# Streaming-window attention and a channel mix on one core: sink scores in column tiles, small copies spread over engines, zero matmuls limited to the start

## The chip, the cores and the metric

The kernel runs on one core of one Trainium2 chip. The metric is the device time of one execution in microseconds (us). The engines are TensorE (PE, and PEld for its weight loads), VectorE (DVE), ScalarE (ACT), GpSimd (POOL) and SyncE (SP), which issues nearly all DMAs.

## The reference

Four batches, eight heads, 768 positions, head size 64. Each position attends to the 128 positions up to itself and to the first four positions of its batch (the sinks). The heads side by side give rows of 512 numbers, which go through a channel mix.

```python
scores = scale * np.matmul(q, k.transpose(0, 1, 3, 2))
keep = is_sink | in_window                       # pos < 4, or 0 <= rel < 128
a = np.exp(scores - max); a = a / (sum(a) + 1e-09)
x = np.matmul(a, v)                              # -> (B, S, 512)

xk = mu_k * x + (1.0 - mu_k) * x_prev            # x_prev: one position earlier
xr = mu_r * x + (1.0 - mu_r) * x_prev
k = np.maximum(xk @ w_k, 0.0)                    # 512 -> 1024
v = k * k @ w_v                                  # 1024 -> 512
r = 1.0 / (1.0 + np.exp(-(xr @ w_r)))            # 512 -> 512
return r * v
```

Inputs and output are float32; the kernel multiplies in bf16.

## The kernel before

The work is cut into 12 units `u`, each 256 positions of a batch: `b, T = divmod(u, 3)`. A unit passes through four functions. Names in brackets are the tiles and lines of the profile.

- `prepare(u)`: keys and queries are loaded in float32 (`ks`, `qs`), cast to bf16 (`kb`, `qb`, L526 and L529), transposed on TensorE (L550) and copied out of PSUM (`kt`, `qt`, L560). For later units (keys from unit 4, queries from unit 8) a DMA transposes instead (L537). Values are cast to `vb` (L575). For the first unit of a batch the keys of the four sinks are copied into `ksink` (L588), and their values, spread over partitions by a matmul (L594), into `vsink` (L598).
- `attend(u)`: sink scores (L611) for units with T > 0; window scores two head pairs at a time (L635), the two heads of a pair in the two 64-row halves of the array; exponentials (`e`, L657; `es`, L619); masks (L671); values (L682, L694); division by the sum (`rec`, L707; `x`, L710).
- `mix(u)`: x is transposed (L733) and copied out (`xt`, L744); the difference to the position before (`td`, L758); four `xk` and four `xr` (L768).
- `ffn(u)`: key products (L818), relu (`rl`, L827), its square (`kk`, L831), gates (L841) and tanh (`th`, L847), products with w_v (L859, for the last 128 rows L788), output (`ob`, L868) and its store (L875). The sigmoid is made from a tanh, and w_v is halved for it when it is cast.

Every piece of work is declared by `P.op(engine, cost, emit, ...)` with what it reads, writes, takes from a pool and holds. The pools of buffers (`ks`, `kt`, `e`, `bank`, ...) set how far ahead work may run. The order on each engine is written out by hand in `ORDER`, as numbers of operations. `Plan.schedule()` walks the five lists with the costs, chooses a buffer for each taking, and merges the lists into one program. It also finds stretches in which TensorE would wait and puts zero matmuls there (L879, on the tile `warm`), as long as its own clock is below `P.fill_until`. The engines themselves run their lists in order and wait on semaphores.

The weights w_k (halves a and b), w_r and w_v (halves a and b) are loaded once, in float32, into tiles of their own, and cast in ten pieces on VectorE (L503, L501). In SyncE's list the loads of unit 0 come first, then keys and queries of unit 1, both halves of w_k, values of unit 1, queries of unit 2, w_r, keys of unit 2, and then w_v's halves between queries and keys of unit 3.

Of the kernel before, what the change touches and what calls it, by code (L numbers as in the profile page):

```python
# [17 lines left out]
CAST = {"k": "ACT", "q": "ACT"}  # L18

CAST0 = {"k": "DVE", "q": "DVE"}  # L20
EVAC0 = {"k": "ACT", "q": "DVE", "x": "ACT"}
# [14 lines left out]
LOADS = ("kq0", "v0", "kq1", "wka", "v1", "wkb", "wr", "wva", "wvb")  # L36
WCAST = ("DVE",) * 10
VCAST = ("DVE", "POOL")
# [6 lines left out]
        92, 89, 98, 105, 95, 116, 108, 113, 128, 141, 124, 119, 131, 137, 103, 148, 134, 157,  # L45
        155, 168, 219, 211, 207, 212, 220, 208, 160, 176, 165, 171, 183, 189, 215, 193, 200,
        223, 180, 216, 225, 237, 298, 186, 290, 302, 291, 303, 299, 294, 248, 295, 227, 235,
        231, 263, 232, 228, 260, 306, 266, 318, 240, 256, 245, 251, 310, 276, 269, 311, 283,
        326, 329, 308, 321, 314, 343, 315, 370, 378, 352, 366, 371, 379, 332, 367, 374, 382,
        337, 375, 384, 359, 348, 386, 396, 387, 421, 390, 274, 444, 391, 452, 445, 453, 426,  # L50
        407, 448, 456, 394, 449, 457, 460, 399, 464, 404, 465, 415, 462, 410, 430, 472, 499,
        578, 437, 468, 474, 504, 469, 525, 583, 526, 537, 485, 538, 533, 509, 529, 534, 530,
        477, 553, 482, 488, 493, 545, 511, 564, 518, 549, 541, 546, 543, 550, 601, 609, 605,
        602, 556, 610, 606, 567, 631, 613, 561, 572, 614, 617, 587, 619, 621, 594, 629, 622,
        634, 625, 639, 626, 642, 677, 689, 678, 681, 663, 690, 682, 645, 707, 685, 650, 686,
        695, 701, 670, 718, 705, 702, 693, 697, 710, 698, 760, 715, 761, 756, 768, 757, 769,
        721, 726, 764, 742, 765, 772, 749, 740, 784, 780, 774, 781, 795, 834, 830, 835, 842,
        831, 787, 843, 838, 792, 798, 860, 776, 803, 816, 839, 777, 823, 846, 848, 854, 858,
        855, 871, 910, 918, 906, 911, 907, 850, 863, 851, 919, 868, 936, 874, 914, 879, 915,
        930, 892, 924, 899, 931, 926, 947, 934, 922, 944, 939, 927, 976, 972, 977, 984, 973,  # L60
        985, 950, 980, 955, 958, 981, 988, 990, 965, 992, 996, 993, 997, 1012, 1000, 1013, 1004,
        1001, 1005, 1008, 1016, 1009, 1020, 1018, 1021, 1028, 1024, 1029, 1025,
    ),
    "DVE": (
        70, 91, 88, 93, 97, 71, 94, 99, 100, 107, 112, 101, 123, 109, 114, 110, 118, 115, 120,
        125, 143, 121, 126, 146, 144, 78, 145, 150, 79, 151, 152, 81, 164, 154, 104, 159, 147,
        175, 170, 161, 80, 162, 177, 166, 178, 167, 172, 153, 173, 82, 83, 202, 195, 196, 210,
        69, 197, 203, 204, 198, 206, 84, 85, 205, 199, 214, 218, 239, 293, 301, 222, 86, 305,
        87, 255, 297, 250, 233, 244, 229, 241, 242, 257, 246, 247, 252, 258, 253, 325, 320, 278,
        312, 279, 285, 280, 287, 322, 286, 327, 323, 328, 331, 316, 281, 289, 288, 282, 354,  # L70
        333, 334, 336, 369, 373, 338, 355, 339, 377, 361, 381, 362, 356, 363, 388, 275, 357,
        392, 364, 365, 398, 358, 403, 447, 451, 414, 455, 400, 459, 401, 409, 405, 406, 466,
        416, 417, 411, 412, 432, 433, 434, 439, 441, 440, 435, 470, 442, 481, 476, 528, 436,
        510, 487, 492, 478, 532, 479, 483, 443, 489, 484, 494, 490, 495, 540, 555, 560, 513,
        536, 514, 520, 516, 515, 522, 521, 547, 551, 523, 571, 517, 566, 557, 558, 604, 524,
        568, 569, 562, 563, 573, 574, 608, 633, 612, 616, 589, 592, 590, 638, 623, 635, 591,
        596, 598, 597, 627, 636, 640, 641, 593, 599, 644, 600, 665, 649, 646, 680, 692, 647,
        684, 651, 652, 714, 666, 688, 709, 672, 667, 674, 703, 668, 675, 673, 711, 725, 699,
        712, 676, 716, 720, 669, 717, 722, 723, 727, 759, 728, 763, 744, 767, 745, 751, 771,
        746, 753, 752, 741, 786, 782, 747, 755, 791, 797, 788, 789, 833, 793, 799, 802, 794,  # L80
        800, 748, 804, 845, 805, 754, 837, 778, 841, 825, 818, 821, 819, 820, 826, 829, 827,
        867, 856, 862, 822, 878, 909, 864, 873, 865, 852, 913, 869, 870, 875, 876, 880, 828,
        881, 917, 921, 894, 943, 897, 932, 895, 938, 896, 901, 905, 902, 945, 903, 940, 941,
        928, 949, 946, 954, 904, 951, 952, 898, 956, 975, 957, 960, 979, 961, 963, 987, 962,
        983, 967, 969, 970, 968, 971, 994, 964, 998, 1003, 1007, 1015, 1011, 1022, 1030, 1026,
    ),
    "ACT": (
        67, 68, 90, 111, 106, 96, 122, 117, 127, 130, 136, 142, 129, 132, 133, 149, 138, 163,
        135, 158, 156, 169, 174, 221, 213, 182, 209, 188, 184, 190, 201, 194, 179, 185, 224,
        181, 217, 226, 238, 187, 243, 292, 262, 300, 304, 296, 254, 249, 236, 264, 259, 265,  # L90
        261, 307, 267, 319, 268, 324, 277, 270, 284, 342, 340, 309, 330, 335, 344, 345, 347,
        353, 372, 380, 368, 420, 425, 383, 376, 360, 498, 418, 349, 385, 397, 422, 503, 423,
        402, 496, 454, 427, 446, 413, 450, 395, 458, 408, 461, 501, 577, 582, 575, 463, 431,
        473, 500, 438, 579, 475, 480, 505, 584, 527, 486, 491, 535, 531, 539, 559, 554, 512,
        519, 565, 580, 542, 544, 653, 570, 655, 603, 611, 607, 657, 632, 615, 618, 588, 659,
        637, 630, 620, 731, 595, 735, 643, 648, 679, 664, 691, 683, 729, 713, 708, 687, 671,
        696, 733, 808, 724, 706, 694, 719, 806, 762, 810, 758, 770, 743, 766, 812, 750, 785,
        790, 775, 773, 801, 882, 796, 836, 832, 844, 866, 861, 840, 817, 824, 849, 847, 884,
        859, 888, 886, 872, 877, 912, 908, 942, 920, 916, 893, 937, 925, 900, 935, 948, 923,
        953, 978, 974, 986, 959, 989, 982, 991, 966, 1014, 1002, 1006, 1010, 1019, 1017,  # L100
    ),
    "POOL": (
        77, 72, 73, 75, 76, 74, 102, 139, 140, 191, 192, 271, 273, 272, 350, 351, 428, 506, 429,
        585, 507, 661, 508, 586, 662, 737, 738, 739, 814, 815, 890, 891,
    ),
    "SP": (
        1, 3, 0, 2, 4, 5, 6, 7, 8, 11, 9, 10, 16, 12, 15, 13, 20, 14, 19, 17, 18, 21, 22, 25,
        23, 234, 24, 30, 341, 28, 35, 346, 313, 29, 317, 26, 33, 27, 389, 38, 34, 40, 31, 419,
        424, 36, 393, 497, 230, 32, 502, 37, 41, 43, 576, 39, 467, 44, 45, 581, 46, 47, 656, 42,
        548, 51, 654, 471, 52, 660, 658, 49, 552, 628, 57, 50, 48, 55, 56, 53, 730, 732, 736,  # L110
        58, 734, 54, 704, 61, 807, 811, 809, 813, 63, 700, 783, 64, 624, 62, 883, 59, 60, 885,
        889, 887, 857, 65, 853, 779, 66, 929, 933, 999, 995, 1023, 1031, 1027,
# [4 lines left out]
class Plan:  # L117
# [17 lines left out]
    def op(self, engine, cost, emit, rank, reads=(), writes=(), take=(), hold=(), port=False,  # L135
           lag=None, service=0.0, descs=128, mode=0):
        self.ops.append(dict(engine=engine, cost=cost, emit=emit, rank=rank, reads=list(reads),
                             writes=list(writes), take=list(take), hold=list(hold), port=port,
                             lag=90.0 if lag is None else lag, service=service, descs=descs, mode=mode))

    def schedule(self):
# [42 lines left out]
        while any(lines.values()):  # L184
# [35 lines left out]
            if o["service"]:  # L220

                descs = o["descs"]
# [9 lines left out]
                flying.append((dma, descs))  # L232
# [39 lines left out]
def kernel(  # L272
# [36 lines left out]
    for name in ("ks", "qs", "vs"):  # L309
        pool(name, 3, [128, 2, H, D] if name == "vs" else [128, H, 2, D], FP32)  # L310
    pool("kb", 3, [128, 2, H, D], BF16)
    pool("qb", 3, [128, 2, H, D], BF16)
    pool("kt", 4, [128, NP, 2, 128], BF16)
    pool("qt", 3, [128, NP, 2, 128], BF16)
# [5 lines left out]
    pool("xk", 3, [128, NC, 256], BF16)  # L320
    pool("xr", 3, [128, NC, 256], BF16)
    pool("kk", 2, [128, NF, 256], BF16)
    pool("rl", 4, [128, 2, 256], BF16)
    pool("th", 4, [128, Dm], FP32)
    pool("ob", 3, [128, Dm], FP32)
    pool("vb", 3, [128, 2, H, D + 1], BF16)
    buf = P.buf

    def tile1(shape, dtype, name):
        return const.tile(shape, dtype, name=name)  # L330


# [144 lines left out]
    def make_sinks():  # L477
        for t in vsink:
            nc.gpsimd.tensor_copy(out=t[0:32, :, D:D + 1], in_=hmask[:, :, D:D + 1])
# [451 lines left out]
```

## Time and profile before

| | |
|---|---|
| median of 4 runs | 172.4 us (172.18 to 172.5) |
| the profiled execution | 172.5 us |
| its span, first to last instruction | 170.8 us |
| granted TensorE clock | 1.00 |
| busy: PE, DVE, ACT, POOL | 162.3, 148.6, 132.5, 24.3 us |
| zero matmuls (L879) | 42, 13.4 us busy |
| sink scores (L611) | 32 matmuls in 8 units |
| value casts on GpSimd (L575) | 22, 811 ns each |
| moved by DMA | 33.8 MB, 198 GB/s over the span |

The profile is of one execution. Busy time of an engine is the union of its instructions' times. Matmuls are pipelined, so an instruction's duration (273 ns for a 256-column matmul) is longer than its distance to the next one; the work on TensorE is better read from the distance of starts. The chain of work that ended last is followed back from the end: each piece is what released the next one, or came before it on its engine. In the timeline, brackets give idle time before an instruction and what ended it.

### The profile page before, as it was taken

Reading aid. Unit: us, or ns where it says so; the run is one execution under the profiler, and the core shown is the slowest. Engines: PE = TensorE matmul, PEld = TensorE weight load, DVE = VectorE, ACT = ScalarE, POOL = GpSimd, SP = SyncE. Lnnn points to the kernel's source line nnn. Section 1 sums busy time; section 2 is a strip of 40 time slices with the busy share of each in tenths; the row PEclk is TensorE's granted clock in tenths of the full one; section 3 lists DMA queues with packets and bytes.
Section 4 is the critical chain, followed back from the end, with each engine's and each line's share of the span. In section 5 each row is a group of like instructions: output and inputs, shape, how many; then the busy total and the mean of one; then the engine's idle time right before and its main releaser. Section 6 shows DMA issues by size and latency. Waiting matters only on the chain.

```text
span 170.8 us, 4214 instructions
## 1 busy us (share of the span) xinstructions
PE 162.3 (95%) x1603; PEld 108.3 (63%) x1624; DVE 148.6 (87%) x372; ACT 132.5 (78%) x219; POOL 24.3 (14%) x47
## 2 busy tenths in 40 slices
PE   7998997899999999999999999999999999999992
PEld 2445585475758567667658668577585775684751
DVE  3496999899899778999999999998999988999632
ACT  3169988899999999999879979978887938654330
POOL 6130040004400020122201200212000402000000
PEclk9999999999999999999999999999999999999999
DMA  4999989998969999999948999977999674030203
GB/s 104 234 273 378 254 268 324 360 311 195 298 175 214 225 255 255 164 258 184 235 86 150 264 230 224 226 135 196 144 271 203 115 212 130 0 125 1 108 15 123
DMA packets 82803, 33.82 MB, mean 198 GB/s; under 512 B 64736, under 2 KB 77280, under 8 KB 82784
## 3 DMA queue, kind: packets, MB, share of 16 engines
q1 hardware_dynamic: 81728, 33.56, 84.3%
q8 instruction: 12, 0.20, 0.5%
q10 hardware_dynamic: 1056, 0.00, 0.3%
q14 instruction: 7, 0.06, 0.1%
HBM read 24.12 MB, written 6.29 MB: 178 GB/s over the span
## 4 chain that ended last, share of the span: by engine, by line
PE 79%; SPq 12%; DMA 5%; issue 1%; ACT 0%; DVE 0%
PE bank L818 23%; PE bank L859 23%; PE bank L841 11%; PE sc L635 6%; DMA ks<-in_k_dram 5%; PE bank L694 5%; SPq L377 5%; SPq L360 4%; PE bank L733 3%; SPq L397 3%; PE bank L682 2%; PE bank L550 2%; PE bank L611 2%; PE bank L788 1%; PE bank L594 0%
## 5 line engine op out<-in xcount | busy, mean ns | idle before, releaser
L657 ACT ACTIVATE e<-sc 128x1024 bf16<-128x1024 f32 (+1 forms) x48 | 44.9, 973 | 5.3 <-PE sc L635 5.3
L818 PE MATMUL bank<-xk,wk_sb 128*128 128x256 bf16 x384 | 49.0, 273 | 0.0
L859 PE MATMUL bank<-wv_h,kk 128*128 128x512 bf16 x173 | 45.4, 379 | 0.6
L818 PEld LDWEIGHTS <-wk_sb 128*128 128x128 bf16 x384 | 35.6, 98 | 7.2 <-issue 0.2
L827 ACT ACTIVATE rl<-bank 128x512 bf16<-128x512 f32 x48 | 27.5, 605 | 9.2 <-PE bank L818 8.6
L575 POOL CAST vb<-vs 128x512 bf16<-128x512 f32 x22 | 17.6, 811 | 111.9 <-DMA vs<-in_v_dram 111.9
L671 DVE TENSOR_TENSOR e<-e,mask 128x1024 bf16<-128x1024 bf16 (+1 forms) x48 | 31.0, 656 | 0.7 <-ACT e L657 0.7
L859 PEld LDWEIGHTS <-kk 128*128 128x128 bf16 x184 | 16.7, 98 | 14.5 <-DVE kk L831 0.2
L841 PE MATMUL bank<-wr_sb,xr 128*128 128x512 bf16 x88 | 23.9, 379 | 0.8 <-DVE wr_sb L503 0.5
L831 DVE TENSOR_TENSOR kk<-rl 128x512 bf16<-128x512 bf16 x48 | 20.1, 432 | 4.6 <-ACT rl L827 4.4
L768 DVE SCALAR_TENSOR_TENSOR xr<-td,mu,xt 128x256 bf16<-128x256 bf16 x48 | 23.2, 499 | 0.1
L768 DVE SCALAR_TENSOR_TENSOR xk<-td,mu,xt 128x256 bf16<-128x256 bf16 x48 | 22.2, 489 | 0.2
L710 DVE TENSOR_TENSOR x<-bank,rec 128x256 bf16<-128x256 f32 x48 | 19.5, 416 | 0.6
L694 PE MATMUL bank<-vb,e 128*128 128x65 bf16 x352 | 18.9, 193 | 0.0
L694 PEld LDWEIGHTS <-e 128*128 128x128 bf16 x352 | 16.8, 97 | 2.8 <-DVE wk_sb L503 0.6
L847 ACT ACTIVATE th<-bank 128x512 f32<-128x512 f32 x24 | 14.1, 599 | 5.0 <-PE bank L841 4.8
L868 DVE SCALAR_TENSOR_TENSOR ob<-th,bank 128x512 f32<-128x512 f32 x23 | 15.6, 680 | 2.1 <-ACT th L847 1.7
L744 ACT COPY xt<-bank 128x512 bf16<-128x512 bf16 x24 | 14.1, 592 | 3.8 <-PE bank L733 3.5
L879 PE MATMUL bank<-warm 128*128 128x512 bf16 x42 | 13.4, 453 | 1.4 <-DVE warm L894 1.3
L841 PEld LDWEIGHTS <-xr 128*128 128x128 bf16 x96 | 9.0, 98 | 8.3 <-DVE wr_sb L503 0.4
L635 PE MATMUL sc<-qt,kt 64*128 64x128 bf16 (+1 forms) x256 | 14.0, 238 | 0.0
L682 PE MATMUL bank<-vsink,es 128*128 128x130 bf16 x64 | 12.5, 220 | 0.5 <-ACT rl L827 0.5
(54 smaller groups left out, 155.9 us busy)
## 6 DMA issues: line engine op xcount, KB each, us to landing
vs<-in_v_dram SPq DMA_DIRECT2D x24, 256.0 KB, 4.5
out_dram<-ob SPq DMA_DIRECT2D x23, 256.0 KB, 3.3
ks<-in_k_dram SPq DMA_DIRECT2D x18, 256.0 KB, 5.0
qs<-in_q_dram SPq DMA_DIRECT2D x7, 512.0 KB, 6.4
qs<-in_q_dram SPq DMA_DIRECT2D x10, 256.0 KB, 4.0
wk<-in_moe_w_k_dram SPq DMA_DIRECT2D x2, 1024.0 KB, 9.4
wv<-in_moe_w_v_dram SPq DMA_DIRECT2D x2, 1024.0 KB, 12.6
ks<-in_k_dram SPq DMA_DIRECT2D x3, 512.0 KB, 9.0
```

The costliest lines, as they stand in the source:

```text
L575: lambda g=g, copy=copy: copy(out=buf["vb", u][:, g, :, 0:D], in_=buf["v", u][:, g, :, :]), rank,
L635: nc.tensor.matmul(out=sc[:, a, o0:o1], lhsT=lhs[rows], rhs=rhs[rows], start=True, stop=True)
L657: nc.scalar.activation(out=buf[ek][:, :, lo:], in_=buf[sck][:, :, lo:], func=AF.Exp, scale=scale)
L671: nc.vector.tensor_tensor(out=at, in0=at, in1=m, op=ALU.mult)
L694: nc.tensor.matmul(out=o[:, g, a, :], lhsT=e[:, a, e0:e0 + 128], rhs=rhs, start=(T == 0 and i == 0), stop=(i == len(blocks) - 1), skip_gro ...
L710: P.op("DVE", dve(256), lambda ok=ok, rk=rk, c=c: nc.vector.tensor_tensor(out=buf["x", u][:, :, 128 * c:128 * c + 128].rearrange("p g (a d ...
L768: nc.vector.scalar_tensor_tensor(out=buf[key][:, c0 + i, :], in0=buf[tk][:, i, :], scalar=mu[w][:, c0 + i:c0 + i + 1], in1=xt[:, c0 + i, t ...
L818: nc.tensor.matmul(out=ps[:, i, :], lhsT=wk_sb[:, c, 128 * f:128 * f + 128], rhs=xk[:, c, :], start=(c == 0), stop=(c == NC - 1), skip_gro ...
L827: P.op("ACT", act(512), lambda psk=psk, rk=rk: nc.scalar.activation(out=buf[rk], in_=buf[psk].rearrange("p (i t) -> p i t", i=2), func=AF. ...
L831: P.op("DVE", dve(512, 0.52), lambda f2=f2, rk=rk: nc.vector.tensor_tensor(out=buf["kk", u][:, 2 * f2:2 * f2 + 2, :], in0=buf[rk], in1=buf ...
L841: nc.tensor.matmul(out=buf[psk], lhsT=buf["xr", u][:, c, 128 * g:128 * g + 128], rhs=wr_sb[:, c, :], start=(c == 0), stop=(c == NC - 1))
L859: nc.tensor.matmul(out=buf[psk], rhs=wv_h[:, f, :], lhsT=buf["kk", u][:, f, 128 * g:128 * g + 128], start=(f == 0), stop=(f == NF - 1))
```

## The change

1. **Sink scores.** `ksink` had one 128-wide block for each pair of heads, nonzero only in that pair's columns; four matmuls accumulated into all 128 partitions. It now has four 32-wide blocks, and each matmul writes its own 32 partitions, so that the four stand in four column tiles of the array. The layouts of `spread`, `hmask` and `vsink` follow.
2. **Engines of casts and evacuations.** Casts, evacuations and relus may now run on one of two or three engines; `CHOICE` names an engine for 61 operations, the others keep their default. In sum: of 22 value casts on GpSimd 13 go to ScalarE and 6 to VectorE; five of ten weight casts go from VectorE to ScalarE; from ScalarE to VectorE go 6 kb, 8 qb (2 come back), 2 kt, 4 qt (1 comes back), 9 xt and 3 relus.
3. **Zero matmuls.** `fill_until` goes from 45000 to 22000 of the planner's nanoseconds.
4. **Buffers.** The float32 weights share three 1 MB buffers, from which each cast frees its part. `qt`, `xk`, `kk`, `rl`, `vb` get one buffer more each. The `kk` buffer is taken with the first relu.
5. **Order.** All five lists of `ORDER` are new. At the head of SyncE's list: unit 0, queries and keys of unit 1, queries of unit 2, both halves of w_k, values of unit 1, keys of unit 2, half the values of unit 2, w_r, the rest of them, both halves of w_v, keys and queries of unit 3. ScalarE issues the two loads of mu behind six instructions and no longer first.
6. **The planner's costs** of load issues are smaller (they are no part of the program but for where zero matmuls and buffers fall).

```diff
-CAST = {"k": "ACT", "q": "ACT"}
-
-CAST0 = {"k": "DVE", "q": "DVE"}
-EVAC0 = {"k": "ACT", "q": "DVE", "x": "ACT"}
+CHOICE = {
+    78: "ACT", 81: "ACT", 82: "ACT", 84: "ACT", 86: "ACT", 88: "DVE", 93: "DVE", 94: "DVE", 96:
...
-LOADS = ("kq0", "v0", "kq1", "wka", "v1", "wkb", "wr", "wva", "wvb")
-WCAST = ("DVE",) * 10
-VCAST = ("DVE", "POOL")
+LOADS = ("kq0", "v0", "kq1", "wka", "wkb", "v1", "wr", "wva", "wvb")
...
     "PE": (
-        92, 89, 98, 105, 95, 116, 108, 113, 128, 141, 124, 119, 131, 137, 103, 148, 134, 157,
-        155, 168, 219, 211, 207, 212, 220, 208, 160, 176, 165, 171, 183, 189, 215, 193, 200,
...
+        89, 92, 105, 95, 98, 103, 116, 108, 113, 131, 137, 141, 128, 124, 119, 155, 134, 157,
+        148, 183, 189, 168, 235, 207, 208, 211, 212, 219, 220, 160, 165, 171, 176, 215, 193,
...
     "DVE": (
-        70, 91, 88, 93, 97, 71, 94, 99, 100, 107, 112, 101, 123, 109, 114, 110, 118, 115, 120,
-        125, 143, 121, 126, 146, 144, 78, 145, 150, 79, 151, 152, 81, 164, 154, 104, 159, 147,
...
+        70, 71, 88, 93, 94, 100, 96, 107, 101, 112, 109, 114, 110, 136, 104, 115, 118, 127, 123,
+        143, 125, 120, 133, 121, 126, 135, 149, 144, 150, 151, 145, 152, 190, 146, 159, 147,
...
     "ACT": (
-        67, 68, 90, 111, 106, 96, 122, 117, 127, 130, 136, 142, 129, 132, 133, 149, 138, 163,
-        135, 158, 156, 169, 174, 221, 213, 182, 209, 188, 184, 190, 201, 194, 179, 185, 224,
...
+        91, 90, 97, 111, 106, 99, 68, 67, 117, 130, 122, 132, 142, 138, 129, 182, 188, 163, 158,
+        184, 78, 156, 174, 169, 81, 139, 209, 221, 236, 213, 179, 185, 194, 201, 181, 191, 187,
...
     "SP": (
-        1, 3, 0, 2, 4, 5, 6, 7, 8, 11, 9, 10, 16, 12, 15, 13, 20, 14, 19, 17, 18, 21, 22, 25,
-        23, 234, 24, 30, 341, 28, 35, 346, 313, 29, 317, 26, 33, 27, 389, 38, 34, 40, 31, 419,
...
+        0, 1, 2, 3, 4, 5, 7, 6, 16, 8, 9, 10, 11, 15, 17, 12, 18, 13, 14, 19, 20, 25, 23, 24,
+        21, 234, 22, 341, 346, 28, 30, 29, 313, 26, 27, 419, 424, 31, 230, 33, 34, 35, 32, 497,
...
-           lag=None, service=0.0, descs=128, mode=0):
-        self.ops.append(dict(engine=engine, cost=cost, emit=emit, rank=rank, reads=list(reads),
+           lag=None, service=0.0, descs=128, mode=0, alts=None):
+        i = len(self.ops)
+        if i in CHOICE:
+            engine = CHOICE[i]
+            cost, emit, port = alts[engine]
+        self.ops.append(dict(alts=alts,engine=engine, cost=cost, emit=emit, rank=rank, reads=list(reads),
...
+    pool("w32", 3, [128, NC, 512], FP32)
-    pool("qt", 3, [128, NP, 2, 128], BF16)
+    pool("qt", 4, [128, NP, 2, 128], BF16)
...
-    hmask = tile1([32, H, D + 1], BF16, "hmask")
-
-    ksink = [tile1([128, NP * 136], BF16, f"ksink{i}") for i in range(2)]
+    hmask = tile1([128, H, D + 1], BF16, "hmask")
+
+    ksink = [tile1([128, NP * 32], BF16, f"ksink{i}") for i in range(2)]
     vsink = [tile1([128, H, D + 1], BF16, f"vsink{i}") for i in range(2)]
...
-        nc.gpsimd.tensor_copy(out=spread[0:NS, 0:4 * H].rearrange("p (h s) -> p h s", s=NS),
-                              in_=ident[0:NS, 0:NS].unsqueeze(1).to_broadcast([NS, H, NS]))
+        for a in range(2):
+            nc.gpsimd.tensor_copy(
+                out=spread[0:NS, :].rearrange("p (c w) -> p c w", w=32)[:, :, 4 * a:4 * a + NS],
+                in_=ident[0:NS, 0:NS].unsqueeze(1).to_broadcast([NS, NP, NS]))
...
+    def cast(out, name, i, cut, rank, writes):
+        key = ("w32", name, i)
+        half = name == "wv"
+
+        def emit(by):
+            if by == "ACT":
+                return lambda: nc.scalar.activation(out=out, in_=buf[key][cut], func=AF.Copy,
+                                                    scale=0.5 if half else 1.0)
+            if half:
+                return lambda: nc.vector.tensor_scalar(out=out, in0=buf[key][cut], scalar1=0.5,
+                                                       scalar2=None, op0=ALU.mult)
+            return lambda: nc.vector.tensor_copy(out=out, in_=buf[key][cut])
+
+        P.op("DVE", dve(1024, 0.52), emit("DVE"), rank, port=True, hold=[key],
+             alts={"DVE": (dve(1024, 0.52), emit("DVE"), True),
+                   "ACT": (act(1024), emit("ACT"), False)},
+             reads=[(name + "32", i)], writes=writes)
 
     for i in range(4):
...
-            by = (CAST if u else CAST0)[name]
-            copy = nc.scalar.copy if by == "ACT" else nc.vector.tensor_copy
...
+            P.op("ACT", act(512), cast(nc.scalar.copy), rank + half,
+                 alts={"ACT": (act(512), cast(nc.scalar.copy), False),
+                       "DVE": (dve(512, 0.52), cast(nc.vector.tensor_copy), True)},
+                 take=[] if half else [(name + "b", rk)],
                  hold=[raw] + ([rk] if half else []), reads=[(name, u, half)],
                  writes=[rk + (half,)])
...
+            P.op("POOL", 760.0, cast(nc.gpsimd.tensor_copy), rank,
+                 alts={"POOL": (760.0, cast(nc.gpsimd.tensor_copy), True),
+                       "ACT": (act(512), cast(nc.scalar.copy), False),
+                       "DVE": (dve(512, 0.52), cast(nc.vector.tensor_copy), True)},
...
-                    nc.tensor.matmul(out=buf[psk][:, 0:256],
-                                     lhsT=ksink[b % 2][:, 128 * c:128 * c + 128],
-                                     rhs=buf["qt", u][:, c, :, :],
-                                     start=(c == 0), stop=(c == NP - 1))
-
-            P.op("PE", 440.0, sink_scores, rank, lag=PE_LAG, take=[("bank", psk)],
+                    nc.tensor.matmul(out=buf[psk][32 * c:32 * c + 32, 0:256],
+                                     lhsT=ksink[b % 2][:, 32 * c:32 * c + 32],
+                                     rhs=buf["qt", u][:, c, :, :], start=True, stop=True)
+
+            P.op("PE", 150.0, sink_scores, rank, lag=PE_LAG, mode=2, take=[("bank", psk)],
...
+                P.op("ACT", act(512), evacuate(nc.scalar.copy), r,
+                     alts={"ACT": (act(512), evacuate(nc.scalar.copy), False),
+                           "DVE": (dve(512, 0.54), evacuate(nc.vector.tensor_copy), True)},
...
+            P.op("ACT", act(512), relu, rank + f2,
+                 alts={"ACT": (act(512), relu, False), "DVE": (dve(512), relu_dve, False)},
+                 take=[("rl", rk)] + ([] if f2 else [("kk", ("kk", u))]),
+                 hold=[psk] + ([("kk", u)] if f2 else []), reads=[psk + (0,), psk + (1,)],
+                 writes=[rk])
...
-    P.fill_until = 45000.0
+    P.fill_until = 22000.0
```

## The prediction

> **What bounds the kernel now.** I read the busy shares first, then the busy time by stages, then the chain that ended last, then TensorE's own timeline of the first 32 us.
>
> ```profile
> PE 162.3 (95%) x1603; PEld 108.3 (63%) x1624; DVE 148.6 (87%) x372; ACT 132.5 (78%) x219; POOL 24.3 (14%) x47
> ...
> 20.00:30.00 10.00, 8.97 (x106) 6.44 (x104) 10.00 (x24) 8.74 (x15) 1.74 (x2) 1.00 0.94 276
> 30.00:40.00 10.00, 9.10 (x87) 6.33 (x87) 9.28 (x23) 9.51 (x16) 0.00 (x0) 1.00 1.06 314
> 40.00:50.00 10.00, 9.95 (x120) 6.21 (x119) 9.24 (x24) 9.62 (x18) 3.85 (x6) 1.00 0.96 239
> ```
>
> The columns of the stages are length, then busy PE, PEld, DVE, ACT, POOL, then PEclk and DMA. From 40 us on TensorE is full. Before that it isn't, and there VectorE is (10.00 of 10).
>
> ```profile
> 21.45 9.02 DMA ks<-in_k_dram
> 30.50 0.63 ACT kb L529
> 31.17 0.40 PE bank L550 x4
> ...
> 36.81 0.55 PE sc L635 x12
> 37.36 0.54 PE bank L818 x4
> ...
> 96.50 0.44 PE bank L611 x4
> ```
>
> The chain is one load (the keys of unit 2, landed at 30.47), their cast, and then TensorE alone up to 167.6. The last row is one unit's sink scores. The two above show the price of changing TensorE's tiling: four key products take 0.44 elsewhere and 0.54 behind the row-tiled scores.
>
> ```profile
> 19.66 1.72 PE L879 MATMUL bank<-warm 128*128 128x512 bf16 x7
> 21.31 0.76 PE L635 MATMUL sc<-qt,kt 64*128 64x256 bf16 x12
> 22.01 2.79 PE L818 MATMUL bank<-xk,wk_sb 128*128 128x256 bf16 x24
> ...
> 26.54 0.22 PE L682 MATMUL bank<-vsink,es 128*128 128x130 bf16 x1 [0.49 <-ACT rl L827]
> ...
> 29.13 0.39 PE L841 MATMUL bank<-wr_sb,xr 128*128 128x512 bf16 x1 [0.27 <-DVE wr_sb L503]
> ...
> 31.17 0.40 PE L550 MATMUL bank<-ident,kb 128*128 128x128 bf16 x4 [0.85 <-ACT kb L529]
> ```
>
> The last zero matmul runs at 21 us, although the kernel allows them until its planner's 45. Behind it there are waits.
>
> TensorE's own work, as count times distance from start to start, is 143.3 us: 384 key products at 0.109, 184 products and 96 gates at 0.216, 192 transposes at 0.056, 32 sink scores at 0.110, scores and values 24.2, the rest 2.6. Following its order, only 11.4 of that is done at 31.17; the other 131.9 fill the 136.4 up to 167.6, and nearly all of the 4.5 left over is tiling changes. So after 31 us time can only be won by less TensorE work, and before it by letting work start sooner.
>
> **The change part by part.**
>
> *Head: loads, weight casts, order.* Two numbers carry this: what lands when, and how much TensorE work stands in the order before each thing that must land. From the first half of w_k (landed 17.40) to the second half of w_v (38.23) six MB came in, 3.47 us per MB. Queries 2 (0.5 MB) now go ahead of w_k, so its halves land at about 19.1 and 22.0 (before 17.4 and 20.3). Keys 2 go ahead of w_r: 25.7 for 30.5. w_r slips to 30.1 (28.4) and w_v to 34.5 (33.7); its second half stays at 38, queries 3 slip to 41.5 (35.4). Followed through the new orders, at the rows' durations:
> - First key product: the first w_k cast is now ScalarE's, behind e and qt, and ends at about 20.9; before, the product began at 22.0. The second cast stands on VectorE behind two e and two xr, until 23.3, and the values of unit 1 begin at 25.3.
> - First key product of unit 1: its mix ends on VectorE at 30.35. Before, it ran at 33.42. In order, 12.3 us of work precede it now and 13.4 before: lead 3.07 − 1.06 = 2.0 us.
> - First w_v product: keys 2 no longer stop TensorE at 31, and the gates wait behind key products of unit 1. It starts at 37.6, with 19.5 us of work before it; before, at 37.9 with 17.5. Lead 2.3.
> - After unit 1's first product: 43.35 with 25.2 us done; before, about 45.85. Lead **2.5 us**.
>
> The two mu loads move from the start of ScalarE's queue to behind its sixth instruction, about 10.5. They cost 1.1 us of its queue there (0.49 and 0.59 in the trace), ahead of two e, counted above; landing 3.5 to 4.6 us later, they beat the first xk (about 18). w_v's halves now need a w32 buffer of w_k back (casts at 23 to 24, issues at 22.0 and 24.8 before): nothing on a stream that is full, up to 1 us if SyncE then stands with keys 3 behind. Bounds of the head: 1 us lost to 4 won.
>
> *Zero matmuls.* With the limit at the planner's 22 us none is lost that ran after 21 in this trace. A rule speaks against it: granted clock is 1.00 in every row of stages, and the Trainium skill, "TensorE: Matmul & The Clock Gate", Part 1, says that an idle window of about 3.4 us halves the clock until a busy one has passed. By the row zero; by the rule, if a wait of that length appears, some 3.4 us at half speed, 1.7 us lost. The longest wait in my walk through the new head is 1.9 us, so I take zero.
>
> *Sink scores.* Eight units of four 0.11 us matmuls, 3.5 us. Four column tiles that run together last about one, 0.11 to 0.15 (the row-tiled pairs in the trace start 3 to 4 ns apart), but this is a third tiling: 0.10 to get in and 0.10 out by the rows above. So 0.31 to 0.35 instead of 0.44, and 0.1 less where it stands beside scores. The rule: "TensorEngine Tiling (Array Packing)", Key Properties and Restrictions, lets tiles work in parallel but says that a mode change drains the array and column tiles lose the fast weight load. By the rule's speedup alone (up to four times) eight units would give 2.6 us; by the row of mode changes 0.7 to 1.3. If the four ran in turn, each unit would lose 0.2. I take 0.14 for the six units behind the head: **0.8 us** won; bounds 1.2 lost, 1.5 won.
>
> *Casts and evacuations.* 19 of 22 value casts leave GpSimd (13 to ScalarE, 6 to VectorE); VectorE also takes 6 kb, 6 net qb, 2 kt, 3 net qt, 3 relus and 9 xt from ScalarE, and gives 5 weight casts. In a packed stretch a VectorE instruction costs about 0.08 less than its mean. So 18 casts at 0.335 = 6.0; 5 kt and qt at 0.616 = 3.1; 3 relus at 0.60 (the ob row, f32 from PSUM) = 1.8; 9 xt; less 5 × 0.60 = 3.0. An xt is priced by two rows: 0.34 like td (bf16, plain stride) or 0.616 like qt (PSUM source, scattered write). I take 0.34, since only the write differs in kind: 3.1 (5.5). VectorE goes from 138.0 us of packed work to **149.0** (151.5). ScalarE goes from 126 to 122.5. Back comes what GpSimd cost VectorE: an xr takes 0.83 at most beside a value cast against 0.48, in all some 3 us of stretching, most of which goes. The deeper pools (qt, xk, kk, rl, vb) cost nothing and absorb lateness.
>
> TensorE alone would then end at 167.6 − 2.5 − 0.8 = 164.3. But the last unit's first key product needs VectorE's last xk, and the new order puts that 12.1 us of TensorE work before the end (8.7 before). Counting from kk of unit 1, at 40.8 with 34.1 done, VectorE has 107.3 us of packed work up to that xk. TensorE wants it at 152.1, so VectorE would have to be 96% full for 111 us. Before, that stretch was 86% full; its fullest ten-microsecond stages reached 94 to 95%, with GpSimd in the way. At 95% the xk comes at 153.8, 1.7 us late. I take stalls of 1.0.
>
> **Sum**: profiled execution 172.5 (span 170.8 and 1.7 around it) − 2.5 − 0.8 + 1.0 = 170.2. The median of the runs is 172.4, 0.1 lower: **170.1**.
>
> **The rivals.**
> 1. *VectorE becomes the bound, slower than before.* Price: (107.3 / fill) against 111.3. At 92% fill the last xk comes at 157.4, and with 17.2 us behind it (12.1 TensorE, 3.4 last store, 1.7 around the span) the time is 174.6. It decides from 93.8% downwards. For it: 11 us more on an engine that already ran 9.3 of 10 while TensorE was the bound, in a fixed order in which an evacuation that waits for a bank holds back everything. Against: an engine that is late finds its inputs ready; deeper pools; GpSimd out of the way. 0.23.
> 2. *No stall at all*: VectorE keeps 97%, and sink scores gain beside scores: 172.4 − 2.5 − 1.3 = 168.6. 0.22.
> 3. *The head does not move*: loads are the limit whatever their order (DMA 0.94 to 1.13 busy from 10 to 40), w_r and w_v later eat what keys 2 win, and only the sink scores remain, against some stalling: 172.4 − 0.8 + 0.6 = 172.2. 0.08.
>
> **How the numbers follow.** The forecast has 0.47: 169.3 to 171.5. The range 168.2 to 174.2 adds rival 2 and most of rival 1, leaving out the worst fills. Less than 0.2% (0.3 us) can't be told from no change here: faster needs under 172.05. That holds for the forecast, rival 2 and a little of rival 3: 0.71. Same: 0.06. Slower: 0.23.
>
> **What would show it.** TensorE's first key product of unit 1 at about 30 rather than 33.4; no wait on kb of unit 2; the first w_v product at 37 to 38 with 2 us more done before it; no zero matmul after 22 and clock 1.00; sink scores of four overlapping matmuls, about 0.3 a unit; VectorE busy about 157, over 9.5 of 10 in every stage to 150; GpSimd under 8. I am wrong if TensorE waits for xk or td by more than 4 us after 45 (rival 1), if one wait in the head passes 3 us, or if the sink scores' matmuls stand 0.1 apart.

## The result and the profile after

The changed kernel takes 171.5 us (median), the kernel before 172.4 in the same series: ratio 0.9939, 95% interval 0.9927 to 0.9951. So it is faster, by 0.6%, where the prediction had 1.3% (170.1 us); 171.5 stands at the upper edge of its forecast, 169.3 to 171.5. Runs over 1.5% above the fastest of the same kernel are left out of the times and ratios here and below.

The profiled execution of the changed kernel took 171.62 us. Its page, cut to the span, the busy time and the granted clock:

```profile
span 169.9 us, 4166 instructions
...
PE 158.9 (94%) x1584; PEld 105.9 (62%) x1602; DVE 153.7 (90%) x403; ACT 129.1 (76%) x208; POOL 12.5 (7%) x31
...
PEclk9996599999999999999999999999999999999999
...
PE 84%; DVE 10%; ACT 3%; issue 1%; ACTq 0%; DVEq 0%
```

The last line is the chain that ended last: the 5% of DMA and the 12% of SyncE's queue are gone, and VectorE has come in with 10%. The line above it holds the surprise. Of the 40 slices (4.2 us each), the fourth and fifth have a granted TensorE clock of 0.6 and 0.5, where the kernel before has 9 in every slice. Before, the chain and the stage from 10 to 20 us were:

```profile
PE 79%; SPq 12%; DMA 5%; issue 1%; ACT 0%; DVE 0%
...
10.00:20.00 10.00, 8.92 (x95) 5.15 (x95) 8.63 (x29) 8.88 (x15) 1.29 (x4) 1.00 1.13 335
```

After, by stages (columns: length, busy PE, PEld, DVE, ACT, POOL, clock, DMA share, GB/s):

```profile
10.00:20.00 10.00, 7.92 (x88) 5.27 (x87) 8.32 (x23) 7.85 (x12) 1.13 (x3) 0.70 1.10 325
20.00:30.00 10.00, 7.67 (x98) 6.14 (x97) 9.58 (x24) 8.94 (x16) 0.00 (x0) 0.96 1.06 269
30.00:40.00 10.00, 9.07 (x95) 6.22 (x94) 9.96 (x26) 10.00 (x16) 0.00 (x0) 1.00 1.11 341
40.00:50.00 10.00, 9.89 (x95) 5.67 (x95) 9.96 (x26) 9.37 (x17) 1.11 (x3) 1.00 0.73 164
```

The trace's clock records give the edges: half speed from 13.91 to 20.74 us, 6.83 us long. VectorE runs at 9.96 of 10 from 30 on, TensorE at 9.89 from 40 on: both are full together.

This is TensorE's timeline of the changed kernel in the stretch ahead of the fall (start, duration, instruction; in brackets the wait before it):

```profile
10.63 0.51 PE L654 MATMUL sc<-qt,kt 64*128 64x256 bf16 x8 [0.38 <-DVE e L690]
11.07 0.36 PE L713 MATMUL bank<-vb,e 128*128 128x65 bf16 x6
11.66 0.36 PE L713 MATMUL bank<-vb,e 128*128 128x65 bf16 x6 [0.24 <-DVE e L690]
12.38 0.40 PE L569 MATMUL bank<-ident,qb 128*128 128x128 bf16 x4 [0.36 <-ACT qb L544]
12.94 0.40 PE L569 MATMUL bank<-ident,qb 128*128 128x128 bf16 x4 [0.16 <-DVE qb L544]
13.54 0.72 PE L752 MATMUL bank<-ident,x 128*128 128x128 bf16 x4 [0.20 <-DVE vsink L618]
```

and in that of the kernel before, over the same microseconds:

```profile
10.67 0.40 PE L550 MATMUL bank<-ident,kb 128*128 128x128 bf16 x4
10.91 1.03 PE L879 MATMUL bank<-warm 128*128 128x512 bf16 x3
11.90 0.50 PE L635 MATMUL sc<-qt,kt 64*128 64x256 bf16 x8
12.34 0.61 PE L879 MATMUL bank<-warm 128*128 128x512 bf16 x2
12.78 0.59 PE L694 MATMUL bank<-vb,e 128*128 128x65 bf16 x12
13.21 1.24 PE L879 MATMUL bank<-warm 128*128 128x512 bf16 x5
```

Before, ten zero matmuls (`warm`, L879) lie between 10.9 and 14.5 and no wait remains. After, there is none in that stretch and five waits, none over 0.4 us, 1.3 us in sum. The last transposes take 0.72 instead of 0.40: the clock has just been halved.

The marks that the prediction set up, from the same timeline:

```profile
24.46 1.92 PE L839 MATMUL bank<-xk,wk_sb 128*128 128x256 bf16 x16 [1.09 <-DVE wk_sb L513]
...
31.57 0.39 PE L839 MATMUL bank<-xk,wk_sb 128*128 128x256 bf16 x2
...
39.64 1.03 PE L888 MATMUL bank<-wv_h,kk 128*128 128x512 bf16 x4
```

The first key product of unit 1 comes at 31.57 (forecast 30.35, before 33.35), the first w_v product at 39.64 (forecast 37.6). A sink unit beside scores, again after:

```profile
92.30 0.39 PE L752 MATMUL bank<-ident,x 128*128 128x128 bf16 x4
92.62 0.29 PE L631 MATMUL bank<-qt,ksink 128*32 128x256 bf16 x4
92.84 0.62 PE L654 MATMUL sc<-qt,kt 64*128 64x256 bf16 x12
```

Four transposes are 0.22, so the sink matmuls start 0.10 late, at the change of tiling, and the scores follow 0.22 later. The four matmuls themselves start 3 to 4 ns apart. A unit is 0.32, of which the scores would have paid 0.10 anyway; it was 0.44.

### The profile page after: what moved, and what is told of

It reads as the page before. It is cut to its first block, busy times and chain, and to the rows that moved or that the text cites. A ratio compares the mean times of both kernels' runs of the same rounds, so it can differ in the third digit from the quotient of the medians.

```text
span 169.9 us, 4166 instructions
## 1 busy us (share of the span) xinstructions
PE 158.9 (94%) x1584; PEld 105.9 (62%) x1602; DVE 153.7 (90%) x403; ACT 129.1 (76%) x208; POOL 12.5 (7%) x31
## 4 chain that ended last, share of the span: by engine, by line
PE 84%; DVE 10%; ACT 3%; issue 1%; ACTq 0%; DVEq 0%
PE bank L839 23%; PE bank L888 23%; PE bank L870 12%; PE sc L654 7%; PE bank L713 6%; PE bank L908 3%; PE bank L752 3%; PE bank L569 2%; PE bank L701 2%; DVE e L690 2%; DVE xk L789 2%; DVE x L729 1%; PE bank L631 1%; PE bank L809 1%; DVE qt L577 1%
## 5 line engine op out<-in xcount | busy, mean ns | idle before, releaser
L839 PE MATMUL bank<-xk,wk_sb 128*128 128x256 bf16 x384 | 50.5, 273 | 1.4 <-DVE wk_sb L513 1.1
L849 ACT ACTIVATE rl<-bank 128x512 bf16<-128x512 f32 x45 | 26.2, 607 | 10.3 <-PE bank L839 7.8
L690 DVE TENSOR_TENSOR e<-e,mask 128x1024 bf16<-128x1024 bf16 (+1 forms) x48 | 30.0, 637 | 0.6 <-ACT e L676 0.6
L789 DVE SCALAR_TENSOR_TENSOR xr<-td,mu,xt 128x256 bf16<-128x256 bf16 x48 | 22.4, 474 | 0.0
L876 ACT ACTIVATE th<-bank 128x512 f32<-128x512 f32 x24 | 14.8, 619 | 7.8 <-PE bank L870 7.7
L861 DVE TENSOR_TENSOR kk<-rl 128x512 bf16<-128x512 bf16 x48 | 19.3, 414 | 0.2 <-ACT rl L849 0.2
L654 PE MATMUL sc<-qt,kt 64*128 64x128 bf16 (+1 forms) x256 | 14.9, 247 | 1.1 <-ACT kt L577 0.7
L654 PEld LDWEIGHTS <-kt 64*128 64x128 bf16 x256 | 9.5, 97 | 7.3 <-issue 4.8
L761 ACT COPY xt<-bank 128x512 bf16<-128x512 bf16 x15 | 8.8, 587 | 5.4 <-PE bank L752 4.6
L779 DVE TENSOR_TENSOR td<-xt 128x512 bf16<-128x512 bf16 x24 | 10.1, 419 | 0.1
## 6 DMA issues: line engine op xcount, KB each, us to landing
w<-in_moe_w_v_dram SPq DMA_DIRECT2D x2, 1024.0 KB, 10.5
```

The costliest lines, as they stand in the source:

```text
L654: nc.tensor.matmul(out=sc[:, a, o0:o1], lhsT=lhs[rows], rhs=rhs[rows], start=True, stop=True)
L690: nc.vector.tensor_tensor(out=at, in0=at, in1=m, op=ALU.mult)
L789: nc.vector.scalar_tensor_tensor(out=buf[key][:, c0 + i, :], in0=buf[tk][:, i, :], scalar=mu[w][:, c0 + i:c0 + i + 1], in1=xt[:, c0 + i, t ...
L839: nc.tensor.matmul(out=ps[:, i, :], lhsT=wk_sb[:, c, 128 * f:128 * f + 128], rhs=xk[:, c, :], start=(c == 0), stop=(c == NC - 1), skip_gro ...
L849: nc.scalar.activation(out=buf[rk], in_=buf[psk].rearrange("p (i t) -> p i t", i=2), func=AF.Relu)
L861: P.op("DVE", dve(512, 0.52), lambda f2=f2, rk=rk: nc.vector.tensor_tensor(out=buf["kk", u][:, 2 * f2:2 * f2 + 2, :], in0=buf[rk], in1=buf ...
```

## The experiments

The question was where a little over half of the expected gain stayed. Theory A: the halved clock, because the new order leaves TensorE thin between 10 and 17 us. Theory B: VectorE, full in every stage. A has two branches: theory C, that the new order took the zero matmuls away, and rival D, that the lower limit did.

**1. The change, with ten zero matmuls put into the head.** `EXTRA` counts them by operation; all lie between 11 and 17 us.

```diff
+EXTRA = {113: 1, 131: 2, 137: 1, 141: 1, 128: 3, 134: 2}
...
+                for _ in range(EXTRA.get(i, 0)):
+                    self.fill(self.buf[self.ops[i]["take"][0][1]])
```

> The changed kernel with ten more zero matmuls (0.22 us each) in the stretch from 11 to 17 us, where TensorE waits for unit 1, each written into the bank that the next operation overwrites. Theory A (cold clock): the granted clock fell to one half from 13.9 to 20.7 us because the window before it held too little TensorE work, and this cost 1.0 to 1.5 us of the head. Then the clock stays at 1.00 and the time falls from 171.5 to 170.0 to 170.6. Theory B (VectorE is the bound, 100% busy from 30 to 110 us): the clock may stay up, but the time stays at 171.3 to 171.7, since VectorE's queue decides.

Measured: 170.69 us, 0.9908 (0.9886 to 0.993); its profiled execution 170.32; 0.1 above the range of theory A, and below that of theory B. Its stages:

```profile
10.00:20.00 10.00, 7.99 (x104) 5.07 (x104) 9.40 (x26) 8.80 (x14) 1.20 (x4) 1.00 1.11 324
20.00:30.00 10.00, 7.87 (x105) 6.31 (x105) 9.53 (x25) 9.14 (x17) 0.00 (x0) 1.00 1.08 274
30.00:40.00 10.00, 9.77 (x91) 6.38 (x90) 10.00 (x25) 10.00 (x15) 0.00 (x0) 1.00 1.11 340
```

The clock is 1.00 and from the first key product up to about 138 us TensorE's operations run 1.6 us earlier than in the changed kernel; at the end 1.3 are left. More work made the kernel shorter. That is what theory A said. With six runs the interval just touches that of the change (0.9927 to 0.9951); experiment 9 and the change's own runs, sorted by their clock (further down), agree with it. This kernel is the base of the experiments that are marked "on 1".

**2. The kernel before, with its zero matmuls cut off at 10 of the planner's us.**

```diff
-    P.fill_until = 45000.0
+    P.fill_until = 10000.0
```

> The kernel before with no zero matmul behind its planner's 10 us (24 instead of 44 in the program). Theory A: the clock falls to one half somewhere between 10 and 21 us and the time rises from 172.4 to 173.2 to 174.0. Theory B: the zero matmuls do nothing for the time, 172.2 to 172.6.

Measured: 173.07 us, 1.0045 (1.0023 to 1.0067), 0.6 us slower than before and 0.1 under theory A's range; its profiled execution 173.19. The stage from 10 to 20:

```profile
10.00:20.00 10.00, 7.11 (x80) 4.49 (x79) 8.81 (x29) 8.52 (x15) 1.28 (x4) 0.85 1.13 337
```

The same kind of loss, made in the old kernel by nothing but missing zero matmuls: every run had a mean clock of about 0.98 or 0.99, and its records show half speed from 17.09 to 20.51. In the window ahead of it TensorE waits 1.15 us for a cast of keys (L529) and three times 0.2 to 0.3 us.

**3. The change with the limit back at 45.**

```diff
-    P.fill_until = 22000.0
+    P.fill_until = 45000.0
```

> The changed kernel with the limit for zero matmuls back at 45000 (27 instead of 22 in the program; the five more stand behind the first key product of unit 0, about 23 us, and before the scores of unit 2, about 30). Theory C: the cold clock comes from the new order, in which nothing was put into TensorE's waits between 10 and 17 us, and not from the lower limit; then the clock falls as often as in the changed kernel and the time is 171.2 to 171.8. Rival D: the lower limit is the cause; then the clock stays up and the time is that of the kernel with zero matmuls from 11 to 17 us, 170.3 to 170.9.

Measured: 171.94 us, 0.9954 (0.9925 to 0.9982), 0.1 above theory C's range, clock 0.96 to 0.99 in eleven of twelve runs, half speed from 14.16 to 24.40 in the profiled one. The program has 27 zero matmuls then, not 22, but none in the 4 us ahead of the fall. So the limit is not the cause, rival D falls, and theory C stands: the planner places zero matmuls where its own times show a gap of over 0.3 us, and in the new order it placed none between 10 and 17.

**4. The change with less work on VectorE.** The masks of the odd head pairs are left out from unit 3 on, 10.0 us of VectorE.

```diff
-            P.op("DVE", dve(width, 0.52), masked, r, hold=[ek], ...
+            P.op("DVE", dve(width, 0.52), (lambda: None) if u > 2 and c % 2 else masked, r, hold=[ek], ...
```

> The changed kernel without the mask multiply of every second head pair from unit 3 on (18 VectorE instructions, 10.0 us of packed VectorE work left out). Theory B: at least 1.5 us faster than 171.5, up to 170.0 or below. Theory A: the lost time was lost in the head, before unit 3, and TensorE is full behind it, so within 0.4 us of 171.5 (171.1 to 171.6).

Measured: 171.40 us, 0.9905 (0.9869 to 0.9941). In the profiled execution VectorE falls from 153.7 to 145.5 us:

```profile
PE 160.0 (94%) x1602; PEld 105.9 (62%) x1602; DVE 145.5 (86%) x385; ACT 128.9 (76%) x208; POOL 9.9 (6%) x31
```

and TensorE's operations move by 0.23 us from 66 us on, in an execution with the same 6.83 us of half clock. Eight microseconds less on an engine that is 9.96 full are worth 0.2 there, so VectorE isn't where the 1.4 us went: theory B falls for the change as it ran. Full isn't late. With the full clock it is less sure: the one run of this experiment with a clock of 1.00 took 169.76, less than any run of the change or of 1.

**5. The old sink scores in the changed kernel,** first without zero matmuls added, then **6.** on 1.

```diff
-                    nc.tensor.matmul(out=buf[psk][32 * c:32 * c + 32, 0:256],
-                                     lhsT=ksink[b % 2][:, 32 * c:32 * c + 32],
-                                     rhs=buf["qt", u][:, c, :, :], start=True, stop=True)
+                    nc.tensor.matmul(out=buf[psk][:, 0:256],
+                                     lhsT=ksink[b % 2][:, 128 * c:128 * c + 128],
+                                     rhs=buf["qt", u][:, c, :, :],
+                                     start=(c == 0), stop=(c == NP - 1))
```

> The changed kernel with the old sink scores (four accumulating 128-column matmuls, old layouts), all else the same. If the sink scores' saving reaches the end (0.12 us a unit, and 0.10 more for the four units where they stand right before row-tiled scores): 0.7 to 1.2 us slower than the changed kernel, 172.2 to 172.7. If VectorE hides it (theory B): within 0.2 of 171.5.

Measured: 171.14 us, 0.9923 (0.9899 to 0.9946), not slower than the change and outside both expectations. Its profiled execution had full clock throughout, and so had three of its six runs. The comparison is confounded by the clock and says nothing on the sink scores; hence the sixth.

> The changed kernel with the ten zero matmuls from 11 to 17 us and the old sink scores, against the same with the new ones (170.7). If each unit's saving reaches the end: 0.8 to 1.2 us slower, 171.5 to 171.9. If part of it is taken by waits that were covered before, as the traces of the two so far suggest (0.2 a unit won, 0.4 lost at about 60 us): 171.0 to 171.3. If it is hidden: 170.5 to 170.9.

Measured: 171.14 us, 0.9928 (0.9909 to 0.9947), against 170.69 for 1: 0.45 us, while the intervals overlap. The two traces, both at clock 1.00, say where it goes. From 69 us on TensorE's operations come 0.22 us earlier with the column tiles behind each of five units, 1.08 us in sum, and that is the 0.44 of the old unit less the 0.22 from the sink matmuls to the scores, as in the result above. But at 65 us they were 0.52 us later: 0.14 of it from the head, and the rest because the column tiles' TensorE waits 0.18 and 0.24 us near 62 us. At 150 us 0.56 is left.

**7. On 1, 19 value casts back on GpSimd.**

```diff
-    ... 139: "ACT", 140: "DVE", ... 191: "ACT", 192: "ACT", ...
+    ... 139: "POOL", 140: "POOL", ... 191: "POOL", 192: "POOL", ...
```

> The changed kernel with the ten zero matmuls, and all 19 value casts of units 1 to 11 back on GpSimd, at the place that their start has in the plan. By an exclusive lock on the port that GpSimd and VectorE share (each cast of 0.8 us stops VectorE): 15 us more for VectorE, at least 3 us slower than 170.7. By the rows of the trace (a few VectorE instructions stretched, 3 us in all, VectorE not the bound): 170.4 to 171.3.

Measured: 171.51 us, 0.9952 (0.9932 to 0.9971), 0.8 us slower than 1 and 0.2 above the second expectation. GpSimd's casts and the mix that makes an xk on VectorE, in this run, as groups (the number behind the busy time is the mean in ns), and then with the shortest, median and longest in ns:

```profile
L712 DVE SCALAR_TENSOR_TENSOR xk<-td,mu,xt 128x256 bf16<-128x256 bf16 x48 | 23.9, 523 | 0.1
L514 POOL CAST vb<-vs 128x512 bf16<-128x512 f32 x22 | 21.7, 990 | 95.2 <-DMA vs<-in_v_dram 95.1
...
L712 DVE SCALAR_TENSOR_TENSOR xk<-td,mu,xt x48: 458/481/840, 17.0 to 154.0; 128x256 bf16<-128x256 bf16 x48
L514 POOL CAST vb<-vs x22: 611/802/3409, 22.9 to 143.7; 128x512 bf16<-128x512 f32 x22
```

and that mix in 1:

```profile
L793 DVE SCALAR_TENSOR_TENSOR xk<-td,mu,xt 128x256 bf16<-128x256 bf16 x48 | 22.7, 500 | 0.1
```

A mix takes 523 ns instead of 500, and VectorE is busy for 154.7 us instead of 153.3 although it has six casts fewer. "SBUF — State Buffer" of the Trainium skill, in its section on who interferes with whom, calls the port that the two engines share an exclusive lock: the one that issues first has it for the whole instruction, and the other is blocked. The first expectation took VectorE for the blocked one each time, 19 casts of 0.8 us, an estimate of 15 us. The trace shows both cases, which fits such a lock: a mix lasts up to 0.84 us beside a cast, and the longest cast, 3.41 us for 0.61 alone, lies beside nine VectorE instructions that keep their usual times. GpSimd's casts are stretched by 22 × (0.990 − 0.611) = 8.3 us in sum; VectorE by an estimated 3.4 (1.4 busier, with six casts of about 0.335 fewer). TensorE waits 0.9 us for two of the casts. So most of the price fell on the engine that is seldom waited for, and 0.8 us is what reached the end.

**8. On 1, nine evacuations behind 40 us (eight xt, one relu) back on ScalarE.**

```diff
-    ... 277: "DVE", ... 353: "DVE", 360: "DVE", ... 519: "DVE", ...
+    ... 277: "ACT", ... 353: "ACT", 360: "ACT", ... 519: "ACT", ...
```

> The changed kernel with the ten zero matmuls, and eight xt evacuations and one relu (those behind 40 us) back on ScalarE. VectorE has 3.3 us less, ScalarE 4.4 more. If VectorE's load costs the end time: 0.5 us or more faster than 170.7. If TensorE alone sets it and either engine has room: 170.4 to 171.0. If ScalarE's order now holds back e or th: slower, up to 172.5.

Measured: 172.98 us, 1.003 (1.001 to 1.0049), 2.3 us slower than 1 and 0.5 above the worst expectation; the whole gain is gone. Nothing is overfull: in the stage from 110 to 120 all three engines have time.

```profile
110.00:120.00 10.00, 9.38 (x102) 5.62 (x101) 8.94 (x25) 7.38 (x14) 2.02 (x2) 1.00 0.75 186
```

In 1 TensorE has 10.00 there. ScalarE's timeline shows the order at work:

```profile
113.79 0.60 ACT L799 ACTIVATE th<-bank 128x512 f32<-128x512 f32 x1 [1.20 <-PE bank L793]
114.28 1.51 ACT L599 ACTIVATE e<-sc 128x768 bf16<-128x768 f32 x2
115.66 0.61 ACT L684 COPY xt<-bank 128x512 bf16<-128x512 bf16 x1
```

ScalarE waits 1.20 us for a gate's bank, then does two exponentials, and only then the xt that was moved. VectorE waits 1.4 us for an xt (td at L702) and TensorE 0.59. At equal work done, counted by TensorE's weight loads, this run is 0.7 us behind 1 at 102 us, 2.3 at 124 and 2.7 at the end, so this stretch costs more than half. So the nine evacuations seem to pay because they come sooner in VectorE's list than in ScalarE's, not because ScalarE lacks time; other places in ScalarE's list weren't tried. A waiting instruction costs what is queued behind it.

**9. Another set of zero matmuls, fourteen in place of ten.**

```diff
-EXTRA = {113: 1, 131: 2, 137: 1, 141: 1, 128: 3, 134: 2}
+EXTRA = {113: 1, 131: 2, 137: 1, 141: 1, 128: 2, 155: 1, 134: 2, 235: 2, 211: 2}
```

> The changed kernel with fourteen zero matmuls in TensorE's waits up to 25 us: the places of the ten, and two each before the sink scores of unit 2 and the second key product of unit 0, where the longest waits stood. If the cold clock explains the spread of the changed kernel (170.0 at a mean clock of 1.00, 171.5 at 0.98), every run is now at 0.99 or more and the median is 170.2 to 170.7, with no run over 171.5. If zero matmuls in a wait delay the work behind them: 170.8 to 171.3.

Measured: 170.47 us, 0.9902 (0.9871 to 0.9934), clock 1.00 in all six runs. It has the lowest median, ahead of both kernels, but can't be told from 1. Two of its six runs took 171.5 us at that clock, so the clock isn't the whole of the spread; the rest stays open.

**10. On 1, the old order of the loads at SyncE's head** (the other orders stay).

```diff
-        0, 1, 2, 3, 4, 5, 7, 6, 16, 8, 9, 10, 11, 15, 17, 12, 18, 13, 14, 19, 20, 25, 23, 24,
+        0, 1, 2, 3, 4, 5, 7, 6, 8, 9, 10, 11, 16, 12, 15, 13, 20, 14, 19, 17, 18, 25, 23, 24,
```

> The kernel with ten more zero matmuls, and at the head of SyncE's list the old order of loads: w_k before queries of unit 2, w_r before keys of unit 2, w_v between queries and keys of unit 3, values of unit 2 last. If the order of loads carries the gain of the head: keys 2 land at 30.5 for 25.5 and values 2 at about 41 for 27 to 31, and TensorE's order waits for them: 3 to 8 us slower than 170.7. If the head is set by VectorE and not by loads: within 1 us of 170.7.

Measured: 184.86 us, 1.0728 (1.0689 to 1.0767), 14 us slower than 1 where 3 to 8 were expected. TensorE's longest waits (for whom: sum, times, longest):

```profile
PE bank L573 <- ACT qb L548: 7.7, 2, 7.0
PE bank L843 <- ACT kt L581: 3.1, 1, 3.1
```

Queries 2 land at 23.55 instead of 15.21, and TensorE's list has their transposes ahead of nearly everything; in that hole the clock falls as well, for four windows of 3.41 us in all. The gain of the load order can't be told from that of TensorE's order: each is built on the other.

**11. On 1, the two mu loads first in ScalarE's list, as before the change.**

```diff
-        91, 90, 97, 111, 106, 99, 68, 67, 117, ...
+        67, 68, 91, 90, 97, 111, 106, 99, 117, ...
```

> The kernel with ten more zero matmuls, and the two mu loads first in ScalarE's queue again. Moving them back delays queries 0 by 1.1 us (landed 5.8 before, 4.7 in the changed kernel) but takes 0.25 us of issuing off the chain at 9.3 us. If the early landing reaches the first key product: 0.5 to 1.0 us slower than 170.7. If the first unit is held by later loads (queries and keys of unit 1): 170.4 to 170.9.

Measured: 172.60 us, 1.0016 (0.9987 to 1.0044), 1.9 us slower than 1, twice what was expected at most. The first keys land at 4.50 instead of 3.75 us and the first queries at 6.07 instead of 4.56, and everything up to w_k stays 0.6 to 1.5 us later. The rest is the clock again:

```profile
20.00:30.00 10.00, 8.28 (x93) 6.25 (x93) 9.13 (x24) 8.60 (x15) 0.00 (x0) 0.83 1.02 260
```

Half speed from 21.86 to 25.28. Four runs of it with the full clock have a median of 172.0, so the loads' delay is about 1.3 us and the clock the other 0.6.

## Why the prediction was right in direction and wrong in size

Point by point, in its own steps. Experiment 1 is the change as the prediction assumed it to run: with the clock at 1.00.

- **Head, loads.** Right. In the changed kernel w_k's halves landed at 18.27 and 21.90, keys 2 at 25.50, w_r at 29.82, w_v at 34.12 and 37.35, queries 3 at 40.97, each within 0.9 us of its forecast. Rival 3 (the head doesn't move) is out with the clock full, as the next point shows.
- **Head, TensorE's lead of 2.5.** Too high by 0.6 with the clock full, and nearly gone without. The first w_v product of unit 1 (four matmuls), before, in the changed kernel and in experiment 1:

```profile
45.14 1.03 PE L859 MATMUL bank<-wv_h,kk 128*128 128x512 bf16 x3
...
44.48 0.81 PE L888 MATMUL bank<-wv_h,kk 128*128 128x512 bf16 x3
...
42.88 1.03 PE L892 MATMUL bank<-wv_h,kk 128*128 128x512 bf16 x4
```

Counted by weight loads, since a few matmul records are missing, the kernel before has 0.3 us more work done there. So the lead is 45.14 − 42.88 − 0.3 = 1.9 us with the full clock and 0.3 in the profiled execution of the change. In experiment 1 this product ends at 43.91, for a forecast of 43.35: the first key product of unit 1 was early (29.97 for 30.35), and the first w_v product late (38.04 for 37.6; the one before starts at 37.74, not 37.9). What held the stretch between them back isn't settled.
- **Zero matmuls, zero. This is the step that failed.** It held that the lower limit loses none, as the last one ran at 21 us, and judged the clock by the longest single wait of the walk, 1.9 us, where the window is 3.4. Two errors lie in that. The ten that ran between 10.9 and 14.5 were lost, by the order and not by the limit; the walk through the new order had them nowhere and didn't ask what filled the waits before. And no long wait was needed: five waits of 0.16 to 0.38 us between small matmuls were enough. The rule of "TensorE: Matmul & The Clock Gate", Part 1, speaks of an idle window; here a window in which TensorE was 66% busy was enough, and the measurement decides. The prediction priced it at 1.7 us for one window. Measured: two windows at half speed, 1.6 us at the first key product and 1.3 at the end (the profiled executions 171.62 and 170.32), 0.8 between the medians of the change and of experiment 1.
- **Sink scores, 0.8.** The price of one unit was right (0.32 for the forecast 0.31 to 0.35). In the traces of 1 and 6 five units brought 0.22 each, as they stand beside scores: 1.1 us from the head on, where the forecast had 0.14 for each of six. What failed is that all of it was to reach the end: 0.4 went into waits near 62 us, and 0.56 is left at the end of the traces, 0.45 between the medians, where the intervals overlap.
- **Stalls, 1.0.** Near: experiment 1 has 1.9 from the head and 1.1 from the sink scores, and its last matmul starts only 2.2 us earlier than before, so 0.8 were given back. Of these 0.4 are the waits near 62 us; experiment 4 traces 0.2 to VectorE; the rest isn't settled.
- **VectorE as the bound (rival 1).** Its load was sized nearly right (busy 153.7, forecast 157) and so was its fill, over 96%; that TensorE would then wait was not. The waits that the changed kernel's profile lists for TensorE behind 45 us come to 0.3 us, and none is for VectorE. GpSimd's 12.5 us busy, for under 8, made no difference that a run shows.

The sum with the full clock is 172.5 − 1.9 − 1.1 + 0.8 = 170.3, which is experiment 1's profiled execution; the 1.3 us of half clock bring it to the 171.6 of the change. That 170.3 lies so near the forecast sum of 170.2 is in part luck: the head brought 0.6 less, and sink scores and stalls came out better by 0.5. The clock also tells the runs of the changed kernel apart: seven with a mean clock of 0.995 or more have a median of 170.3 (170.0 to 171.3), twenty-six below 0.985 one of 171.6 (170.8 to 172.4), while the kernel before had 0.997 or more in every run listed beside the experiments. The forecast was nearly met in the few runs in which the clock held.

## What to carry to other kernels

When a change reorders the start of a kernel, ask of each filler instruction of the old one what it covered, and look for it in the new order: work that computes nothing can still carry the clock. Judge the risk by the whole thin stretch and not by its longest wait, and read the clock row first when a gain comes out too small. A full engine is a bound only if someone waits for it, and moving work to an engine with spare time pays only where its queue isn't waiting just then.

## What the runs showed of the hardware

- **The clock moves in whole windows.** In every trace here each stretch at full or half speed between the first full speed and the end of the work is a multiple of 3.41 us: half speed lasted 6.83 in the change and in experiment 4, 3.41 in experiments 2 and 11, 10.24 in experiment 3. The windows begin at another point in each execution, with first full speed between 3.9 and 7.1 us, which fits that the same program (experiment 5) keeps the clock in some runs and not in others; that the phase is the reason is not shown.
- **Busy share alone doesn't decide.** In the change the window from 10.5 to 13.9, 66% busy with scores, values and transposes, was followed by half speed; that from 20.7 to 24.2, 53% busy with key products above all, was not, and neither was the one from 10.3 to 13.7 in experiment 2, 66% busy as well. What exactly is counted stays open.
- **Changing the tiling costs the same in the third form.** 0.10 us into four column tiles and about 0.11 out of them (the scores start 0.22 behind the sink matmuls, of which the four together are taken to need the 0.11 of one), as with the row tiles of the kernel before (0.10: 0.54 for 0.44).
- **GpSimd and VectorE hold each other up.** In experiment 7 a GpSimd cast of 0.61 us lasts up to 3.41 beside VectorE, and a VectorE mix of 0.48 up to 0.84 beside a cast.
